# A decode step with attention and a gated feed-forward: hand-placed semaphores, three 64 KB regions and a loop on TensorE

## The chip, the core and the metric

The kernel runs on one core of a Trainium2 chip. The metric is the device time of one execution in microseconds (us). Its parts: TensorE (PE in the profile, its weight loads PEld), VectorE (DVE), ScalarE (ACT), GpSimd (POOL), SyncE (SP), which issues most of the loads, and sixteen DMA engines that carry them from HBM into SBUF.

## What is computed

One token `x` of 512 elements goes through an attention over a cache of 32,768 positions (32 query heads, 8 key/value heads, head width 128) and through a gated feed-forward of width 1792; a scalar gate mixes both. All is float32. K and V hold 134 MB each.

```
q = (x @ wq) as 32 heads of 128           # wq 512 x 4096
k, v: 8 heads, each used by 4 query heads  # 32768 x 128 each
p = softmax(q k^T / sqrt(128));  o = p v
a = o @ wo                                 # wo 4096 x 512
b = (silu(x @ w1) * (x @ w3)) @ w2         # w1, w3 512 x 1792, w2 1792 x 512
g = sigmoid(sum(x * gate_w))
out = g * a + (1 - g) * b
```

## The kernel before

The framework's tile pools place the buffers and set the semaphores; `manual_schedule` keeps each engine's instructions in the order of the program.

**Tiling.** Each K and V head is cut into four tiles of 4 MB: 128 partitions with 32 KB rows, 64 keys of 128 elements each. All tiles, both halves of wq, and w1, w3 and w2 go through the pool `stream` with four buffers (`load`, L67); each load is issued by SP as soon as the buffer's former reader is done. The eight wo pieces of 1 MB have a pool of their own with two buffers (`load_wo`, L269).

**The main loop** (L396) has 37 steps. Step i loads K tile i and, five steps behind (`LAG`), V tile i - 5. A K tile is scored in four parts (`scores`, L183): VectorE transposes a quarter of it in 32x32 blocks into a buffer `kt` (L186), and TensorE multiplies it with the head's query window `win` in four column groups (L193). ScalarE copies the finished scores to SBUF (L200).

**The chain of a head** runs between these parts. `defer` puts a function off by a number of ticks, and there are four ticks in a step: `flip` turns the scores by matmuls with a picking matrix (L209), `top` takes the maximum (L218), `maxima`, `diagonal` and `spread_max` spread it over all partitions (L228 to L240), `softmax` takes the exponentials and their sums (L250), `norm` and `invert` the reciprocal. `values` (L287) multiplies a V tile with the probabilities; after a head's last tile, `heads`, `scaled`, `quarter`, `quartered` and `mix` (L299 to L334) bring the head's output together, multiply it with its wo piece and add it to `acc`.

**Feed-forward.** w1 and w3 are loaded and used in steps 2 to 4 (`ff_rows`, L351). w2 comes last, in three pieces; `ff_down` (L432) multiplies it in two parts, around the last head's `heads`, `scaled` and `mix`. The result is written by L446.

Of the kernel before, what the change touches and what calls it, by code (L numbers as in the profile page):

```python
# [2 lines left out]

# [9 lines left out]
AX = mybir.AxisListType  # L13

P = 128
LAG = 5
# [3 lines left out]
def kernel(  # L20
    ctx: ExitStack,
    tc: tile.TileContext,
    x: bass.AP,
    k_cache: bass.AP,
    v_cache: bass.AP,
    wq: bass.AP,
    wo: bass.AP,
    w1: bass.AP,
    w3: bass.AP,
    w2: bass.AP,  # L30
    gate_w: bass.AP,
    out: bass.AP,
):
    nc = tc.nc
# [5 lines left out]
    NC = D // P  # L40
    SCALE = DH ** -0.5

    NB = 64
    UK = NB * P
    NU = S // UK
    UNITS = HKV * NU
    FR = F // P  # L50
    FJ = F // 4
    assert DH == P and D == 4 * P and REP == 4 and NU == 4 and HKV == 8 and F == FR * P

    const = ctx.enter_context(tc.tile_pool(name="const", bufs=1))
    stream = ctx.enter_context(tc.tile_pool(name="stream", bufs=4))
    proj = ctx.enter_context(tc.tile_pool(name="proj", bufs=2))
    ktp = ctx.enter_context(tc.tile_pool(name="ktp", bufs=2))
    work = ctx.enter_context(tc.tile_pool(name="work", bufs=1))
    ps_s = ctx.enter_context(tc.tile_pool(name="ps_s", bufs=2, space=bass.MemoryType.PSUM))
    ps_o = ctx.enter_context(tc.tile_pool(name="ps_o", bufs=2, space=bass.MemoryType.PSUM))  # L60
    ps_m = ctx.enter_context(tc.tile_pool(name="ps_m", bufs=4, space=bass.MemoryType.PSUM))
    ctx.enter_context(tc.manual_schedule())

    def misc(name):
        return ps_m.tile([P, 512], F32, tag="misc", name=name)

    def load(name, n, src):  # L67
        t = stream.tile([P, NB * DH], F32, tag="stream", name=name)
        nc.sync.dma_start(t[:, 0:n], src)
        return t  # L70


    xs = const.tile([P, NC], F32, name="xs")
    gw = const.tile([P, NC], F32, name="gw")
    nc.sync.dma_start(xs, x.rearrange("a b (p c) -> p (a b c)", p=P))
    nc.scalar.dma_start(gw, gate_w.rearrange("(p c) -> p c", p=P))
    wqd = wq.rearrange("(p c) n -> p (c n)", c=NC)
    QW = NC * HQ * DH // 2
    wq_t = [load(f"wq{b}", QW, wqd[:, b * QW:(b + 1) * QW]) for b in range(2)]


    ident = const.tile([P, P], F32, name="ident")
    make_identity(nc, ident)
    ones = const.tile([P, P], F32, name="ones")
    nc.vector.memset(ones, 1.0)
    sel = ident[:, 0:P:32]
    fold = const.tile([P, 32], F32, name="fold")
    nc.vector.tensor_reduce(fold, ident.rearrange("p (c r) -> p r c", c=4), axis=AX.X, op=ALU.add)

    pick = const.tile([P, 64], F32, name="pick")  # L90
    nc.vector.tensor_copy(
        pick.rearrange("p (g x) -> p g x", g=4), ident.rearrange("p (g x) -> p g x", g=4)[:, :, 0:16]
    )


    quad = const.tile([P, 4, 4, 32], F32, name="quad")
    for q in range(4):
        nc.vector.tensor_copy(quad[:, :, q, :], ident.rearrange("p (x k) -> p k x", k=4))


    xp = const.tile([P, NC, 32], F32, name="xp")
    nc.vector.memset(xp, 0.0)
    nc.vector.tensor_copy(xp[:, :, 0], xs)
    win = const.tile([P, HKV, 4, 32], F32, name="win")
    nc.vector.memset(win, 0.0)
    prob = [const.tile([P, 65 * 16], F32, name=f"prob{b}") for b in range(2)]
    otp = [const.tile([P, REP, 32], F32, name=f"otp{b}") for b in range(2)]
    for b in range(2):
        nc.gpsimd.memset(prob[b][:, 1024:1040], 0.0)
        nc.gpsimd.memset(otp[b], 0.0)  # L110
    acc = const.tile([P, P], F32, name="acc")
    nc.gpsimd.memset(acc, 0.0)
    gate = const.tile([P, 2], F32, name="gate")
    htp = const.tile([P, FR, 32], F32, name="htp")
    nc.gpsimd.memset(htp, 0.0)


    later = {}
    clock = [0]

    def defer(n, fn, *a):
        later.setdefault(clock[0] + n, []).append((fn, a))

    def tick():
        for fn, a in later.pop(clock[0], []):
            fn(*a)
        clock[0] += 1


    def gate_part():  # L130
        pr = work.tile([P, NC], F32, name="gpr")
        nc.vector.tensor_mul(pr, xs, gw)
        sm = work.tile([P, 1], F32, name="gsm")
        nc.vector.tensor_reduce(sm, pr, axis=AX.X, op=ALU.add)
        pg = misc("pg")
        nc.tensor.matmul(pg[:, 0:1], ones, sm, start=True, stop=True)
        nc.scalar.activation(gate[:, 0:1], pg[:, 0:1], AF.Sigmoid)
        nc.vector.tensor_scalar(gate[:, 1:2], gate[:, 0:1], -1.0, 1.0, op0=ALU.mult, op1=ALU.add)


    def queries():
        pq = [misc(f"pq{b}") for b in range(2)]
        for c in range(NC):
            for b in range(2):
                for j in range(4):
                    o = ((c % 2) * HKV + 4 * b + j) * REP * DH
                    nc.tensor.matmul(  # L147
                        pq[b][32 * j:32 * j + 32, :], xp[:, c, :], wq_t[c // 2][:, o:o + REP * DH],
                        start=(c == 0), stop=(c == NC - 1),
                    )  # L150
        for b in range(2):
            qs = work.tile([P, 512], F32, tag="ob", name=f"qs{b}", bufs=2)
            nc.scalar.copy(qs, pq[b])  # L153
            defer(4 * b, spread, b, qs)

    def spread(b, qs):
        rp = ktp.tile([P, 16, P], F32, tag="kt", name=f"rp{b}")
        for r in range(4):
            nc.vector.tensor_copy(  # L159
                rp[:, :, 32 * r:32 * r + 32], qs.rearrange("p (a j) -> p a j", a=16)  # L160
            )
        pt = misc(f"pt{b}")
        for a in range(16):
            nc.tensor.matmul(pt[:, 4 * a:4 * a + 4], rp[:, a, :], sel, start=True, stop=True)  # L164
        if b == 0:
            windows(b, pt)
        else:
            defer(1, windows, b, pt)

    def windows(b, pt):  # L170
        for r in range(4):
            nc.vector.tensor_copy(
                win[32 * r:32 * r + 32, 4 * b:4 * b + 4, :, 4 * r:4 * r + 4],
                pt[32 * r:32 * r + 32, 0:64].rearrange("p (q c j) -> p j c q", q=4, c=4),
            )

    recip = const.tile([P, HKV, REP], F32, name="recip")  # L180
    s_ps, sb, pf = {}, {}, {}

    def scores(i, kin, c):  # L183
        h, m = divmod(i, NU)
        kt = ktp.tile([P, NB * 32], F32, tag="kt", name=f"kt{i}_{c}")
        nc.vector.transpose(  # L186
            kt.rearrange("p (n i) -> p n i", i=32),
            kin.rearrange("p (n c j) -> p c n j", c=4, j=32)[:, c],
        )
        if c == 0:  # L190
            s_ps[0] = ps_s.tile([P, 512], F32, tag="s", name=f"s{i}")
        for g in range(4):
            nc.tensor.matmul(  # L193
                s_ps[0][32 * g:32 * g + 32, :], win[:, h, c, :], kt[:, 512 * g:512 * g + 512],
                start=(c == 0), stop=(c == 3),
            )
        if c == 3:
            if m == 0:
                sb[h] = work.tile([P, 16, 32, NU], F32, tag="sb", name=f"sb{h}", bufs=2)
            nc.scalar.copy(sb[h][:, :, :, m], s_ps[0].rearrange("p (n i) -> p n i", i=32))  # L200
            if m == NU - 1:
                mx = work.tile([P, 2, REP], F32, tag="mx", name=f"mx{h}", bufs=2)
                defer(1, flip, h, 0, mx)


    def flip(h, f, mx):
        pf[h, f] = misc(f"pf{h}_{f}")
        for a in range(8):
            nc.tensor.matmul(  # L209
                pf[h, f][:, 64 * a:64 * a + 64], sb[h][:, 8 * f + a].rearrange("p i m -> p (i m)"), pick,  # L210
                start=True, stop=True,
            )
        if f == 0:
            defer(1, flip, h, 1, mx)
        defer(1, top, h, f, mx)

    def top(h, f, mx):
        nc.vector.tensor_reduce(  # L218
            mx[:, f, :], pf[h, f].rearrange("p (n q) -> p q n", q=REP), axis=AX.X, op=ALU.max
        )  # L220
        if f == 1:
            m1 = work.tile([P, REP], F32, tag="m1", name=f"m1_{h}")
# [145 lines left out]
    def ff_up():  # L368
        defer(0, ff_turn, ff_rows("w3"))
# [105 lines left out]
```

## Time and profile before

| | us |
|---|---|
| median of 3 runs | 703.58 (703.11 to 703.68) |
| span of the profiled execution, first to last instruction | 703.1 |
| PE busy | 469.0 (67%) |
| DVE busy | 323.6 (46%) |
| ACT busy | 69.1 (10%) |
| load queue: 296.23 MB | 98.3% of 16 engines' span |

The profile is of one execution, and its span lies 0.48 us below the median of the timed runs. Instructions are grouped by the line of the kernel (L186 is line 186) and named by what they write and read (`kt<-k`). One float32 matmul of the program stands as two records of PE and two of PEld. "Idle before" a group names what ended the wait. SPq is SP's instruction stream.

### The profile page before, as it was taken

The numbers are of one execution on the slowest core, as the hardware profiler recorded it, in microseconds if no ns is written. First come the engines' busy times: TensorE is split into PE (matmuls) and PEld (weight loads), VectorE is DVE, ScalarE is ACT, GpSimd is POOL, SyncE is SP. The second block draws the span as 40 slices with busy tenths as digits, with TensorE's granted clock in tenths as the row PEclk, the third lists the DMA queues.
The fourth block names the chain that finished last, engine by engine and source line by source line (L and its number), as shares of the span: only waits on it lengthen the run. The fifth ranks groups of instructions, "written<-read, shape, count | busy, mean of one in ns | idle before, by whom it ended". The sixth has DMA issues, their size and how long they took to land.

```text
span 703.1 us, 6918 instructions
## 1 busy us (share of the span) xinstructions
PE 469.0 (67%) x3070; PEld 172.4 (25%) x3070; DVE 323.6 (46%) x269; ACT 69.1 (10%) x175; POOL 1.6 (0%) x12
## 2 busy tenths in 40 slices
PE   2776678776865499655863589635985578557746
PEld 0330143114221043113320143102331142113303
DVE  1079556654743444554543455552653556532000
ACT  0100101210200002000020003000020002000100
POOL 0000000000000000000000000000000000000000
PEclk9756656695787757976688756966678757879878
DMA  8999999999999999999999999999999999999994
GB/s 362 443 430 429 426 437 397 437 428 434 428 432 432 432 432 426 431 432 433 430 424 437 426 436 424 435 427 435 429 433 430 427 433 427 432 431 433 424 422 180
DMA packets 12085, 296.67 MB, mean 422 GB/s; under 512 B 1556, under 2 KB 1560, under 8 KB 2200
## 3 DMA queue, kind: packets, MB, share of 16 engines
q1 hardware_dynamic: 11912, 296.23, 98.3%
q8 instruction: 24, 0.39, 0.2%
q14 instruction: 5, 0.04, 0.0%
q10 hardware_dynamic: 144, 0.00, 0.0%
HBM read 296.23 MB, written 0.00 MB: 421 GB/s over the span
## 4 chain that ended last, share of the span: by engine, by line
DMA 60%; PE 20%; DVE 16%; issue 3%; ACT 0%; SPq 0%; DVEq 0%
DMA k<-in_A_k_cache_dram 47%; DVE kt L186 14%; DMA v<-in_A_v_cache_dram 10%; PE pf L209 7%; PE s L193 6%; DMA wq<-in_A_wq_dram 3%; PE o L287 3%; PE pt L164 1%; PE pa L334 1%; PE pw L351 1%; DVE mx L218 1%; PE pq L147 1%; PE ph L381 0%; PE pb L432 0%; DVE rep L376 0%
## 5 line engine op out<-in xcount | busy, mean ns | idle before, releaser
L186 DVE STREAM_TRANSPOSE kt<-k 128x2048 f32<-128x2048 f32 x128 | 289.8, 2293 | 216.2 <-DMA k<-in_A_k_cache_dram 210.6
L193 PE MATMUL s<-kt,win 128*32 128x512 f32 x1024 | 200.8, 870 | 190.5 <-DVE kt L186 183.5
L287 PE MATMUL o<-v,prob 128*32 128x512 f32 x1024 | 147.8, 729 | 14.0 <-DMA v<-in_A_v_cache_dram 14.0
L193 PEld LDWEIGHTS s<-kt,win 128*32 128x32 f32 x1024 | 25.6, 127 | 298.1 <-issue 161.1
L200 ACT COPY sb<-s 128x512 f32<-128x512 f32 x32 | 35.2, 1099 | 477.5 <-PE s L193 477.5
L287 PEld LDWEIGHTS o<-v,prob 128*32 128x32 f32 x1024 | 37.0, 133 | 113.0 <-issue 91.1
L209 PEld LDWEIGHTS pf<-pick,sb 128*128 128x128 f32 x256 | 52.5, 313 | 24.1 <-issue 24.1
L209 PE MATMUL pf<-pick,sb 128*128 128x64 f32 x256 | 55.3, 406 | 0.0
L218 DVE TENSOR_REDUCE mx<-pf 128x4 f32<-128x512 f32 x16 | 11.1, 692 | 49.6 <-PE pf L209 49.6
L250 ACT ACTIVATE prob<-pf,nm 128x128 f32<-128x128 f32 x64 | 23.4, 496 | 36.3 <-DVE nm L246 36.3
L147 PE MATMUL pq<-wq,xp 128*32 128x512 f32 x64 | 10.9, 846 | 17.8 <-DMA wq<-in_A_wq_dram 17.8
L250 ACT ACTIVATION_READ_ACCUMULATOR prob<-pf,nm 128x1 f32 x64 | 14.7, 229 | 0.0
L307 DVE TENSOR_TENSOR otp<-po,recip 128x4 f32<-128x4 f32 x1 | 0.2, 165 | 31.2 <-PE po L299 31.2
L159 DVE COPY rp<-qs 128x512 f32<-128x512 f32 x8 | 2.8, 416 | 24.0 <-ACT qs L153 24.0
L293 ACT COPY ob<-o 128x512 f32<-128x512 f32 x8 | 4.7, 587 | 76.3 <-PE o L287 76.3
L334 PEld LDWEIGHTS pa<-wo,otp 128*32 128x32 f32 x256 | 9.9, 135 | 6.3 <-issue 6.3
L334 PE MATMUL pa<-wo,otp 128*32 128x128 f32 x256 | 11.2, 328 | 0.0
L317 PEld LDWEIGHTS pk<-on,quad 128*128 128x128 f32 x56 | 9.2, 250 | 7.4 <-issue 7.3
L164 PEld LDWEIGHTS pt<-ident,rp 128*128 128x128 f32 x64 | 9.3, 235 | 3.9 <-issue 3.9
L164 PE MATMUL pt<-ident,rp 128*128 128x4 f32 x64 | 9.5, 285 | 1.1 <-DVE rp L159 1.1
L299 PEld LDWEIGHTS po<-fold,ob 128*128 128x128 f32 x64 | 7.7, 191 | 8.6 <-ACT ob L293 8.6
L317 PE MATMUL pk<-on,quad 128*128 128x4 f32 x56 | 9.8, 299 | 0.0
(57 smaller groups left out, 92.1 us busy)
## 6 DMA issues: line engine op xcount, KB each, us to landing
k<-in_A_k_cache_dram SPq DMA_DIRECT2D x32, 4096.0 KB, 29.8
v<-in_A_v_cache_dram SPq DMA_DIRECT2D x32, 4096.0 KB, 34.0
wq<-in_A_wq_dram SPq DMA_DIRECT2D x2, 4096.0 KB, 17.1
wo<-in_A_wo_dram SPq DMA_DIRECT2D x8, 1024.0 KB, 27.1
w<-in_B_w_dram SPq DMA_DIRECT2D x2, 3584.0 KB, 33.6
w<-in_B_w_dram SPq DMA_DIRECT2D x1, 2048.0 KB, 28.8
w<-in_B_w_dram SPq DMA_DIRECT2D x1, 1024.0 KB, 31.0
w<-in_B_w_dram SPq DMA_DIRECT2D x1, 512.0 KB, 31.7
```

The lines of the kernel that those rows point to most:

```text
L147: nc.tensor.matmul(pq[b][32 * j:32 * j + 32, :], xp[:, c, :], wq_t[c // 2][:, o:o + REP * DH], start=(c == 0), stop=(c == NC - 1),)
L164: nc.tensor.matmul(pt[:, 4 * a:4 * a + 4], rp[:, a, :], sel, start=True, stop=True)
L186: nc.vector.transpose(kt.rearrange("p (n i) -> p n i", i=32), kin.rearrange("p (n c j) -> p c n j", c=4, j=32)[:, c],)
L193: nc.tensor.matmul(s_ps[0][32 * g:32 * g + 32, :], win[:, h, c, :], kt[:, 512 * g:512 * g + 512], start=(c == 0), stop=(c == 3),)
L200: nc.scalar.copy(sb[h][:, :, :, m], s_ps[0].rearrange("p (n i) -> p n i", i=32))
L209: nc.tensor.matmul(pf[h, f][:, 64 * a:64 * a + 64], sb[h][:, 8 * f + a].rearrange("p i m -> p (i m)"), pick, start=True, stop=True,)
L218: nc.vector.tensor_reduce(mx[:, f, :], pf[h, f].rearrange("p (n q) -> p q n", q=REP), axis=AX.X, op=ALU.max)
L250: nc.scalar.activation(prob[h % 2][:, 0:1024].rearrange("p (a n q) -> p a n q", a=16, q=REP)[:, :, 8 * f:8 * f + 8, q], pf[h, f].rearrange ...
L287: nc.tensor.matmul(o_ps[0][32 * t:32 * t + 32, :], prob[h % 2][:, o:o + 32], vt[:, n * P:(n + 4) * P], start=(r == 0 and g == 0), stop=(r ...
L299: nc.tensor.matmul(po[:, 0:REP], ob[:, b * P:(b + 1) * P], fold[:, 4 * b:4 * b + 4], start=(b == 0), stop=(b == 3),)
L317: nc.tensor.matmul(pk[:, 4 * k:4 * k + 4], quad[:, k].rearrange("p q x -> p (q x)"), on, start=True, stop=True)
L334: nc.tensor.matmul(pa[32 * j:32 * j + 32, 0:P], otp[h % 2][:, q, :], wo_t[h][:, q, j * P:(j + 1) * P], start=(q == 0), stop=(q == REP - 1),)
```

## The change

The program is written without the framework's pools (`tile_critical`): every buffer is placed by hand and every wait is a semaphore of the kernel's own.

- **Three regions** `ra`, `rb`, `rc` of 8 MB (64 KB rows) take the place of the four stream buffers. K heads are loaded as two halves, always into ra and rb, V heads as two halves into rc, the last half of V into rb. wq uses rc first; w1 and w3 come last, into ra, then wo as a whole (two halves in ra), then w2 in four pieces in rc.
- **Keys are turned in place**: the transpose writes back into the region it reads, and TensorE reads the turned blocks with a stride of 512 bytes.
- **TensorE's work of a head is a loop** of eight passes, with branches that skip the value part in the first pass. In it, semaphores are counted down again by `take`. A pass does the scores of head h and the values of head h - 1. The other engines' instructions are written out.
- **Queries**: turned by VectorE out of PSUM and spread by sixteen copies. GpSimd copies one head's window into `winbuf` ahead of that head.
- **Softmax**: one flip of 32 half-width matmuls, one maximum, four exponentials.
- **The end**: head outputs, already scaled by the gate, are collected in `otall`. After the last head one matmul spreads them, wo and the first six rows of w2 go into one accumulator, its fold and the rest of w2 into a second, which is the result.

The new code, cut to its core:

```diff
+    def take(sem, n=1):
+        pe.wait_ge(sem, n).then_inc(sem, -n)
...
+    sp.dma_start(rc, wq.rearrange("(p c) n -> p (c n)", c=NC)).then_inc(l_q, 16)
+    sp.dma_start(ra[:, 0:half], kd[0, 0][:, 0:half]).then_inc(l_k0, 16)
+    l_a.by(sp.dma_start(ra[:, half:W], kd[0, 0][:, half:W]), 16)
+    l_b.by(sp.dma_start(rb, kd[0, 1]), 16)
+    for h in range(HKV):
+        if h < HKV - 1:
+            sp.wait_ge(c_k.sem, 2 * h + 1)
+            l_a.by(sp.dma_start(ra, kd[h + 1, 0]), 16)
+        else:
+            sp.wait_ge(c_k.sem, 2 * h + 1)
...
+        if h:
+            sp.wait_ge(c_v.sem, 2 * h)
+        else:
+            sp.wait_ge(c_dve.sem, 1)
+        sp.dma_start(rc, vd[h, 0]).then_inc(l_c, 16)
+        sp.wait_ge(c_k.sem, 2 * h + 2)
+        if h < HKV - 1:
+            l_b.by(sp.dma_start(rb, kd[h + 1, 1]), 16)
+            sp.wait_ge(c_v.sem, 2 * h + 1)
+            sp.dma_start(rc, vd[h, 1]).then_inc(l_c, 16)
+        else:
+            sp.dma_start(rb, vd[h, 1]).then_inc(l_v, 16)
+    sp.wait_ge(c_e.sem, 2)
...
+    sp.wait_ge(c_v.sem, 2 * HKV - 1)
...
+    def scores(m, region):
+        for f in range(2):
+            for c in range(4):
+                take(t_tr)
+                for g in range(4):
...
+                    i = pe.matmul(
+                        s_ps[m][32 * g:32 * g + 32, :], winbuf[:, w:w + 32],
+                        region.rearrange("p (n c i) -> p c n i", c=4, i=32)[:, c, n:n + 16],
...
+        i.then_inc(c_k.sem, 1)
...
+    with nc.Fori(0, HKV, 1, engines=[PE]) as step:
+        take(t_win, 4)
+        scores(0, ra)
+        with pe.If(step > 0):
+            norm()
+            take(l_c, 16)
+            values(0, rc)
+        scores(1, rb)
+        with pe.If(step > 0):
+            take(l_c, 16)
+            values(1, rc)
+        flips()
+        with pe.If(step > 0):
+            heads()
+        maxima()
+
+    def turned(sems, region, f):
+        for s, n in sems:
+            dve.wait_ge(s, n)
+        part = region[:, f * half:(f + 1) * half].rearrange("p (n c j) -> p c n j", c=4, j=32)
+        for c in range(4):
+            dve.transpose(part[:, c], part[:, c]).then_inc(t_tr, 1)
...
+    for h in range(HKV):
...
+        if h:
+            act.wait_ge(c_v.sem, 2 * h)
+            act.copy(ob, o_ps).then_inc(t_ob, 1)
+        dve.wait_ge(c_f.sem, h + 1)
+        dve.tensor_reduce(mx, pf.rearrange("p (a q) -> p q a", q=REP), axis=AX.X, op=ALU.max).then_inc(t_mx, 1)
...
+    take(t_e)
+    for k in range(32):
...
+    pe.wait_ge(l_w2[0], 16)
+    for k in range(W2[1]):
...
+    act.copy(ob, acc).then_inc(t_e, 1)
+    for i in range(1, 4):
+        pe.wait_ge(l_w2[i], 16)
+        for k in range(W2[i], W2[i + 1]):
+            m = rows(htp[:, k, :], w2t[:, k, :], k == W2[1], k == FR - 1)
+            if k == W2[2] - 1:
+                take(t_e)
+                rows(fold, ob, False, False)
+    dve.wait_ge(c_e.sem, n_ff + 3)
+    local.by(dve.tensor_copy(res, pb[:, 0:P]))
+    sp.dma_start(out.rearrange("a b (j e) -> (a b j) e", e=P), res[0:P:32, :]).then_inc(l_out, 16)
```

More of the change, by code (lines that the diff above doesn't have):

```diff
@@ L59 @@
[L59 to L70, printed above, removed]
@@ L73 @@
[L73 to L84, printed above, removed]
@@ L112 @@
[L112 to L138, printed above, removed]
@@ L141, in queries @@
[L141 to L149, printed above, removed]
-                    )
[L151 to L154, printed above, removed]
@@ L170, in windows @@
[L170 to L203, printed above, removed]
@@ L206, in flip @@
[L206 to L222, printed above, removed]
-            nc.vector.tensor_max(m1, mx[:, 0, :], mx[:, 1, :])
-            defer(1, maxima, h, m1)
@@ L279, in values @@
-    def values(v, vt):
-        h, r = divmod(v, NU)
-        if r == 0:
-            o_ps[0] = ps_o.tile([P, 512], F32, tag="o", name=f"o{h}")
-        for g in range(4):
-            for t in range(4):
-                o = 256 * g + 64 * r + 16 * t
-                n = 16 * g + 4 * t
-                nc.tensor.matmul(
-                    o_ps[0][32 * t:32 * t + 32, :], prob[h % 2][:, o:o + 32], vt[:, n * P:(n + 4) * P],
-                    start=(r == 0 and g == 0), stop=(r == NU - 1 and g == 3),
-                )
-        if r == NU - 1:
-            ob = work.tile([P, 512], F32, tag="ob", name=f"ob{h}", bufs=2)
-            nc.scalar.copy(ob, o_ps[0])
-            defer(0, heads, h, ob)
@@ L330, in mix @@
[L330 to L347 removed]
+    SCALE = DH ** -0.5
@@ new lines, in _program @@
+    act.dma_start(xs, x.rearrange("a b (p c) -> p (a b c)", p=P)).then_inc(l_x, 16)
+    act.dma_start(gw, gate_w.rearrange("(p c) -> p c", p=P)).then_inc(l_x, 16)
+    local = count("local")
+    n_xp = local.by(dve.memset(xp, 0.0))
+    local.by(dve.memset(ones, 1.0))
+    c_pool.by(pool.memset(ident, 0.0))
+    pool.wait_ge(c_pool.sem, c_pool.n)
+    n_ident = c_pool.by(pool.affine_select(
+        out=ident, in_=ident, compare_op=ALU.not_equal, fill=1.0, base=0, pattern=[[-1, P]], channel_multiplier=1,
+    ))
@@ new lines, in _program @@
+    dve.tensor_reduce(gsm, gpr, axis=AX.X, op=ALU.add).then_inc(t_x, 1)
+    take(t_x, 2)
+    n_gate = c_q.by(pe.matmul(mc[:, 0:1], ones, gsm, start=True, stop=True))
+    pe.wait_ge(l_q, 16)
+    for c in range(NC):
+        for b in range(2):
+            for j in range(4):
+                o = (c * HKV + 4 * b + j) * REP * DH
+                m = pe.matmul(
+                    pq[b][32 * j:32 * j + 32, :], xp[:, c, :], rc[:, o:o + REP * DH],
+                    start=(c == 0), stop=(c == NC - 1),
+                )
@@ new lines, in values @@
+    def values(r, region):
+        for g in range(4):
+            for f in range(2):
+                for t in range(4):
+                    w = 512 * r + 64 * (2 * g + f) + 16 * t
+                    n = 64 * f + 16 * g + 4 * t
+                    i = pe.matmul(
+                        o_ps[32 * t:32 * t + 32, :], prob[:, w:w + 32], region[:, n * DH:(n + 4) * DH],
+                        start=(r == 0 and g == 0 and f == 0), stop=(r == 1 and g == 3 and f == 1),
+                    )
+        i.then_inc(c_v.sem, 1)
@@ new lines, in flips, with heads @@
+    def flips():
+        take(t_ev, 2)
+        for a in range(16):
+            for s in range(2):
+                i = pe.matmul(
+                    pf[64 * s:64 * s + 64, 64 * a:64 * a + 64], sbuf[:, a].rearrange("p i m -> p (i m)"),
+                    ident.rearrange("p (gf r s q) -> p s r gf q", gf=8, r=2, s=2)[:, s],
+                    start=True, stop=True,
+                )
+        i.then_inc(c_f.sem, 1)
+    def heads():
+        take(t_ob)
+        for b in range(4):
+            i = pe.matmul(
+                mb[:, 0:REP], ob[:, b * P:(b + 1) * P], fold[:, 4 * b:4 * b + 4], start=(b == 0), stop=(b == 3)
+            )
+        i.then_inc(c_h.sem, 1)
@@ new lines, in maxima, with norm @@
+    def maxima():
+        take(t_mx)
+        pe.transpose(ma[0:REP, 0:P], mx, ident).then_inc(c_m.sem, 1)
+        take(t_md)
+        pe.matmul(ma[:, 128:128 + REP], ones[0:REP, :], md, start=True, stop=True).then_inc(c_m.sem, 1)
+    def norm():
+        take(t_p, REP)
+        pe.matmul(mc[:, 0:REP], ones, sums, start=True, stop=True).then_inc(c_n.sem, 1)
+    with nc.Fori(0, HKV, 1, engines=[PE]) as step:
[13 more added lines that the diff above has]
+        maxima()
@@ new lines, in _program @@
+    dve.wait_ge(local.sem, local.n)
+    dve.transpose(htp, hid.rearrange("p (a k) -> p k a", k=FR)).then_inc(t_e, 1)
+    norm()
+    pe.wait_ge(l_c, 16)
+    values(0, rc)
+    n_inv = inverted(HKV - 1)
+    pe.wait_ge(l_v, 16)
+    values(1, rb)
+    act.wait_ge(local.sem, n_hid)
+    act.wait_ge(c_v.sem, 2 * HKV)
+    act.copy(ob, o_ps).then_inc(t_ob, 1)
+    heads()
+    dve.wait_ge(local.sem, n_inv)
+    n = scaled(HKV - 1)
+    dve.wait_ge(local.sem, n)
+    dve.tensor_mul(
+        omask.rearrange("p (a x) -> p a x", x=4),
+        otall.unsqueeze(2).to_broadcast([P, HQ, 4]),
+        dmask.unsqueeze(1).to_broadcast([P, HQ, 4]),
+    ).then_inc(t_e, 1)
@@ L375, in ff_turn, with rows @@
+    pe.wait_ge(l_w2[0], 16)
+    for k in range(W2[1]):
+        t = k % 4
+        i = pe.matmul(
+            acc[32 * t:32 * t + 32, :], htp[:, k, :], w2t[:, k, :], start=False, stop=(k >= W2[1] - 4),
+            skip_group_check=True,
+        )
+    i.then_inc(c_e.sem, 1)
+    act.wait_ge(c_e.sem, n_ff + 2)
+    act.copy(ob, acc).then_inc(t_e, 1)
+    def rows(lhs, rhs, start, stop):
         for j in range(4):
-            nc.vector.tensor_copy(
-                rep[:, 0:FR, 32 * j:32 * j + 32], hid.rearrange("p (a k) -> p k a", k=FR)
-            )
@@ L423 @@
-    w2t = stream.tile([P, FR, D], F32, tag="stream", name="w2")
-    w2d = w2.rearrange("(p k) e -> p k e", k=FR)
-    for a, b in ((0, 8), (8, 12), (12, 14)):
-        nc.sync.dma_start(w2t[:, a:b, :], w2d[:, a:b, :])
-    pb = misc("pb")
-    def ff_down(a, b):
-        for k in range(a, b):
-            for j in range(4):
-                nc.tensor.matmul(
-                    pb[32 * j:32 * j + 32, 0:P], htp[:, k, :], w2t[:, k, j * P:(j + 1) * P],
-                    start=(k == 0), stop=(k == FR - 1),
-                )
@@ L437 @@
-    tick()
-    ff_down(0, 8)
-    tick()
-    tick()
-    tick()
-    nc.vector.tensor_scalar(acc, acc, gate[:, 0:1], None, op0=ALU.mult)
-    ff_down(8, FR)
-    res = const.tile([P, P], F32, name="res")
-    nc.vector.scalar_tensor_tensor(res, pb[:, 0:P], gate[:, 1:2], acc, op0=ALU.mult, op1=ALU.add)
-    nc.sync.dma_start(out.rearrange("a b (j e) -> (a b j) e", e=P), res[0:P:32, :])
+            i = pe.matmul(
+                pb[32 * j:32 * j + 32, 0:P], lhs, rhs[:, j * P:(j + 1) * P], start=start, stop=stop
+            )
```

389 lines of the change are left out of this document (184 added, 205 removed).

## The prediction

> **What bounds the kernel now.** I read the page first (shares, queues, chain), then the chain of waits in order of time, then the timeline and the windows of the end.
>
> ```profile
> span 703.1 us, 6918 instructions
> ...
> PE 469.0 (67%) x3070; PEld 172.4 (25%) x3070; DVE 323.6 (46%) x269; ACT 69.1 (10%) x175; POOL 1.6 (0%) x12
> ...
> q1 hardware_dynamic: 11912, 296.23, 98.3%
> ...
> DMA 60%; PE 20%; DVE 16%; issue 3%; ACT 0%; SPq 0%; DVEq 0%
> ```
>
> The load queue moves 296.23 MB, and its packets fill 98.3% of the span on sixteen engines. TensorE's and VectorE's shares of the chain are mostly work after a landing while later transfers already run. So the rate of the stream comes first. The chain shows landings as the first transposes of K tiles:
>
> ```profile
> 23.38 4.25 PE pq L147 x24
> ...
> 162.20 2.32 DVE kt L186
> ...
> 201.04 2.32 DVE kt L186
> ...
> 242.40 2.32 DVE kt L186
> ...
> 281.40 2.31 DVE kt L186
> ...
> 322.82 2.32 DVE kt L186
> ```
>
> From 201.04 to 322.82 twelve tiles of 4 MB and two wo pieces of 1 MB land, 12.5 tiles: 121.78 / 12.5 = 9.742 us each, 430.5 GB/s. All of wq (8.39 MB) had landed at 23.38. What follows up to the last V tile is 296.23 - 8.39 - 3.67 (w2) = 284.17 MB, 67.75 tiles, 660.0 us: due at 683.4.
>
> ```profile
> 687.58 6.59 PE L287 MATMUL o<-v,prob 128*32 128x512 f32 x32 [3.38 <-DMA v<-in_A_v_cache_dram]
> ...
> 694.25 0.59 ACT L293 COPY ob<-o 128x512 f32<-128x512 f32 x1 [37.74 <-PE o L287]
> ...
> 698.52 1.49 PE L432 MATMUL pb<-w,htp 128*32 128x128 f32 x48
> ...
> 700.08 0.35 DVE L445 SCALAR_TENSOR_TENSOR res<-pb,gate,acc 128x128 f32<-128x128 f32 x1 [0.70 <-PE pb L432]
> 700.46 0.65 SPq L446 DMA_DIRECT2D out_dram<-res  x1
> ```
>
> It landed at 687.58: the stream lost 4.2 us in all. Of these, 2.4 went early: the tile turned at 162.20 is 14 tiles after wq (nine of K, three of V, w1, w3 and the first wo), due at 159.8. The last 1.8 are spread over 525 us. Behind the last V tile w2 is still streaming:
>
> ```profile
> 695.00:696.00 1.00, 1.00 (x12) 0.98 (x16) 0.02 (x1) 0.00 (x0) 0.00 (x0) 1.00 0.15 61
> 696.00:697.00 1.00, 1.00 (x42) 1.00 (x42) 0.14 (x1) 0.00 (x0) 0.00 (x0) 1.00 0.00 0
> ```
>
> The last column is GB/s: the bytes end before 696. The span runs 7.1 us longer, because the values of that V tile (until 694.25), heads, wo and w2 follow one another on TensorE. So the change can gain on the start, on 4.2 us of losses and on 7.1 us of tail, unless it moves the rate.
>
> **The change, part by part.**
>
> *64 KB rows: taken at 0.* The bytes stay, the packets of K, V and wq halve. The wo pieces have 8 KB rows: four tiles with one of them (201.04 to 242.40) took 41.36 us, four without (242.40 to 281.40) 39.00. So 1 MB in four times as many packets took 2.36, no more than a quarter of a tile, 2.44; a packet's cost doesn't show. Longer rows than 32 KB the trace doesn't have; I allow 1% of the stream, -7 to +7. [...]
>
> *Start: -0.4.* wq is SP's first load, in one piece; xs goes to ACT's queue.
>
> ```profile
> 0.74 0.39 SPq L75 DMA_DIRECT2D xs<-in_A_x_dram  x1
> ...
> 1.19 0.89 SPq L69 DMA_DIRECT2D wq<-in_A_wq_dram  x2
> ...
> 2.00:3.00 1.00, 0.00 (x0) 0.00 (x0) 1.00 (x6) 0.45 (x1) 0.25 (x1) 1.00 2.01 526
> ```
>
> The row of SP's xs goes, so wq lands at about 22.95. Bytes flow 1 us after an issue (1.19 to the window from 2.00).
>
> *Three regions of 8 MB for four tiles of 4 MB.* A region takes 19.48 us. In SP's order K(0,0) has landed at 42.4 (first half 32.7), K(0,1) 61.9, K(1,0) 81.4, V(0,0) 100.9, K(1,1) 120.4, if each is issued in time. SP now waits for a whole region to be used up, and behind its waiting instruction stand all later loads: behind K(1,0) stands V(0,0), though rc is free long before; behind V(0,1) all of head 2. The prices:
>
> ```profile
> L186 DVE STREAM_TRANSPOSE kt<-k 128x2048 f32<-128x2048 f32 x128 | 289.8, 2293 | 216.2 <-DMA k<-in_A_k_cache_dram 210.6 <-PE s L193 5.5
> ...
> L200 ACT COPY sb<-s 128x512 f32<-128x512 f32 x32 | 35.2, 1099 | 477.5 <-PE s L193 477.5
> ...
> L218 DVE TENSOR_REDUCE mx<-pf 128x4 f32<-128x512 f32 x16 | 11.1, 692 | 49.6 <-PE pf L209 49.6
> ...
> L147 PE MATMUL pq<-wq,xp 128*32 128x512 f32 x64 | 10.9, 846 | 17.8 <-DMA wq<-in_A_wq_dram 17.8
> ...
> L240 PE MATMUL pb<-md,ones 4*128 4x4 f32 x16 | 3.2, 271 | 0.0
> L228 PE MATMUL pr<-ident,m 128*4 128x128 f32 x8 | 2.9, 360 | 1.0 <-DVE m L223 1.0
> ...
> L233 DVE TENSOR_REDUCE mr<-pr 4x1 f32<-4x128 f32 x8 | 2.0, 247 | 0.5 <-PE pr L228 0.4
> ...
> L172 DVE COPY win<-pt 32x64 f32<-32x64 f32 x8 | 1.8, 221 | 7.3 <-PE pt L164 7.3
> L235 DVE TENSOR_SCALAR md<-ident,mr 4x4 f32<-4x4 f32 x8 | 1.7, 217 | 0.3
> ...
> L246 DVE TENSOR_SCALAR nm<-pb 128x4 f32<-128x4 f32 x8 | 1.1, 134 | 0.3 <-PE pb L240 0.2
> ...
> L365 DVE TENSOR_TENSOR hid<-sg,pw 128x448 f32<-128x448 f32 x1 | 0.6, 622 | 0.0
> ```
>
> TensorE has two speeds here, and warms in a series: the same sixteen value matmuls took 3.64 or 6.33, sixteen records of flips 3.68 or 1.9, a group of scores 1.93, from the fourth on 1.06.
>
> ```profile
> 327.14 3.68 PE L209 MATMUL pf<-pick,sb 128*128 128x64 f32 x16
> ...
> 355.25 3.64 PE L287 MATMUL o<-v,prob 128*32 128x512 f32 x32
> ...
> 386.97 1.93 PE L193 MATMUL s<-kt,win 128*32 128x512 f32 x8 [9.11 <-DVE kt L186]
> ...
> 393.52 1.06 PE L193 MATMUL s<-kt,win 128*32 128x512 f32 x8 [0.26 <-DVE kt L186]
> ...
> 640.08 3.79 PE L209 MATMUL pf<-pick,sb 128*128 128x64 f32 x32
> ...
> 677.86 6.33 PE L287 MATMUL o<-v,prob 128*32 128x512 f32 x32 [8.73 <-DMA v<-in_A_v_cache_dram]
> ```
>
> First region, ra: wq 22.95, queries 10.9 (now after the whole of wq), two turns out of PSUM (0.6 each, as L365), sixteen small copies like L172 (3.5): 38.6. Eight transposes 18.3, last scores at most 1.9: K(1,0) is issued at 58.8 and flows from 59.8, before K(0,1) has landed (61.9). No stall, 2 us to spare.
>
> First value region, rc, the tightest: K(0,1) at 61.9, transposes 18.3, scores 1.1, copy 1.1, flips, the maximum 1.4 (twice L218), its spreading 1.2 (L228, L233, L235, L240, L246) and 0.4 for hops. Flips are now 64 records with half-width weights: between half of 2 x 3.79 and the whole, 3.8 to 7.6, I take 3.8, since the narrow weights load in step with their columns. That is 89.2; only then does VectorE turn K(1,0), landed since 81.4. Plus 18.3, scores 1.1, norm 0.4, values 7.3 (2 x 3.64): 116.3, V(0,1) flows from 117.3, against 120.4. No stall, 3.1 us to spare (-0.7 with long flips).
>
> Later heads have more. From K's landing to V's issue 18.3 + 1.1 + 0.4 + 7.3 + 1.0 = 28.1 us, while two regions cover 39.0; and from V's second landing values, flips, maximum and spreading take 14.1, plus 1 for heads, against 19.5 until the next K. DVE's in-place turn I take at 2.29, as its strided reading stands in L186 already and only the writing becomes strided; nothing shows a gain, and up to 10.9 / 8 = 1.4 us more per transpose is hidden.
>
> *Tail: -3.7.* wo, now 8 MB, lands ahead of w2 (8.5 us of stream), so V's last values, heads and spreading (28 us before the last byte) are covered, and the wo matmuls follow their half: 3.6 to 6.3 of those 8.5. After the last row of w2 there remain eight records (0.25, from the row with 48), the copy 0.35, hops 0.15 and the out DMA from 700.46 to 703.1, 2.64: 3.4 instead of 7.1. If TensorE were cold here, 2 us of it come back.
>
> *TensorE's loop, own semaphores, one accumulator: 0.* The loop names TensorE alone and has no barrier with other engines, and fewer small matmuls only free TensorE, which isn't the bound. Two waits are new. A head's scores wait for four small GpSimd copies of its query window (mean 0.13 us for GpSimd's twelve instructions now); behind them TensorE's whole head is queued, but they run while VectorE turns the first eighth, 2.3 us. On ScalarE the exponentials stand behind the copy of `ob`, which waits for the last head's values; their own input, the spread maximum, comes after those values anyway. If either cover were gone, it would be under 1 us a head, inside the 10.9 above. On SP, wo waits for both feed-forward matmuls on ra, over 25 us ahead of its turn in the stream.
>
> **The sum.** 22.95 + 287.84 MB in 68.63 tiles, 668.6, + 1.8 of lost stream (the early 2.4 gone with the longer queue) + tail 3.4 = 696.8 us of span, against 703.1. The median of the runs, 703.58, lies 0.48 above this profiled execution's span, so **697.3 us**.
>
> **Rivals.**
>
> *Cold TensorE on the first pass (slower).* In the first value chain TensorE idles before the flips and again before K(1,0). Cold, it costs 1.8 on scores (two groups at 1.94 for 1.06), 5.4 on values (12.7 for 7.3), and on flips 3.6, or 10.9 if half-width weights gain nothing (14.7 for 3.8): 10.8 to 18.1 against 3.1 of slack. The stream then stands 7.7 to 15.0 us, 705.0 to 712.3; in the middle 708.7. It is slower as soon as the chain grows by more than 10.8, and every further us is paid whole. For it: 677.86. Against it: eight groups of scores precede each, and the third warms them.
>
> *The jump back stalls TensorE (slower).*
>
> ```profile
> q8 instruction: 24, 0.39, 0.2%
> ...
> gw<-in_gate_w_dram ACTq DMA_DIRECT2D x1, 2.0 KB, 2.0
> ...
> w<-in_B_w_dram SPq DMA_DIRECT2D x1, 512.0 KB, 31.7
> ```
>
> The program itself arrives by DMA in 24 packets, and a loop goes back to code it has left. A jump then costs a small load, between 2.0 us (gw) and 31.7, if it queues like w2's piece. From the end of one head's spreading there are 34.7 us until its scores have to be done, of which warming scores take 11.1: a stall up to 23.6 us is hidden. At 31.7 it costs 8.1 in each of seven heads, 754 us. [...]
>
> *In-place turns are slower.* At twice 2.29 the chain of 28.1 becomes 46.4, 7.4 over its cover in seven heads: 749. It decides from 3.65 us each.
>
> *The gain is eaten (no change).* Handing over 8 MB regions loses 5 to 7 us more, by the long flips, a skipped branch at head 0 and a cold tail: 702.2 to 705.0.
>
> *The rate rises by 1% with long rows (faster):* 690.4.
>
> **How the numbers follow.** Forecast 0.56, rate 0.08, no change 0.10, cold first pass 0.15, jump 0.06, in place 0.05. A measurement here tells 0.2% from no change: faster means below 702.2, slower above 705.0. Faster 0.64, same 0.10, slower 0.26. The range 691 to 709 takes in the forecast with its bounds, half of the higher rate and the cold pass up to its middle; jump, in-place turns and those other halves, some 0.2, stay out.
>
> **What would show it.** Right: load queue full from 2 us on, first halt none around 118 to 122, turns of 2.3 us, the bytes ending near 693 and out issued 1 us later. Wrong: a hole in the GB/s line at 120, turns over 3.6 us, a first score group that waits for nothing after each head, or slices well off 430 GB/s.

## The result, and the profile after

The change makes the kernel faster: 698.65 us median (697.92 to 699.55, four runs) against 703.63 (703.11 to 704.51) on the same chip, a ratio of 0.993 with a 95% interval of 0.9916 to 0.9944. The forecast was 697.3. The profiled execution took 698.76 us, its span is 696.7; forecast was a span of 696.8. That hit is partly luck, as the stages below show: a halt that wasn't forecast and a faster stream that wasn't either cancel. The gain in time was forecast at 6.3 us and is 5.0.

The page of the changed kernel (busy time by engine, GB/s in 40 slices of 17.4 us, queues):

```profile
span 696.7 us, 6587 instructions
...
PE 374.5 (54%) x2944; PEld 104.0 (15%) x2944; DVE 307.9 (44%) x208; ACT 38.7 (6%) x94; POOL 7.1 (1%) x41
...
GB/s 399 412 453 411 430 419 369 421 425 467 433 421 421 421 478 425 421 421 433 463 429 421 421 433 463 429 421 421 433 463 429 422 421 433 426 459 426 425 419 276
...
q1 hardware_dynamic: 6056, 296.23, 98.6%
q8 instruction: 6, 0.10, 0.1%
```

Same bytes, half the packets, and 6 packets of code where there were 24. The stream is full but for the seventh slice (369), the start and the end. Landings, as the first transposes of regions in the timeline (start, duration, what ended the wait):

```profile
61.89 17.66 DVE L295 STREAM_TRANSPOSE rb<-rb 128x2048 f32<-128x2048 f32 x8 [4.46 <-DMA rb<-in_A_k_cache_dram]
...
122.02 8.89 DVE L295 STREAM_TRANSPOSE rb<-rb 128x2048 f32<-128x2048 f32 x4 [10.79 <-DMA rb<-in_A_k_cache_dram]
...
162.69 17.66 DVE L295 STREAM_TRANSPOSE ra<-ra 128x2048 f32<-128x2048 f32 x8 [4.36 <-DMA ra<-in_A_k_cache_dram]
...
317.81 17.66 DVE L295 STREAM_TRANSPOSE ra<-ra 128x2048 f32<-128x2048 f32 x8 [7.30 <-DMA ra<-in_A_k_cache_dram]
...
511.31 8.89 DVE L295 STREAM_TRANSPOSE rb<-rb 128x2048 f32<-128x2048 f32 x4 [21.04 <-DMA rb<-in_A_k_cache_dram]
```

K(0,1) lands at 61.9 to the tenth as worked out. K(1,1) comes 1.6 late (120.4 was due), K(2,0) 3.3 late (159.4). From then on the stream makes good: from 317.81 to 511.31 five pairs of regions take 193.50, 38.70 us a pair, where two regions were put at 38.96 and the kernel before took 39.00 for its four tiles without wo.

Half of the 3.3 us (1.66, by the first experiments below) went in the first head's flips and what follows them:

```profile
82.17 0.65 PE L248 MATMUL psum<-ident,sbuf 128*64 128x64 f32 x14 [0.82 <-PEq L106]
87.68 3.04 PE L248 MATMUL psum<-ident,sbuf 128*64 128x64 f32 x50 [4.85 <-issue]
...
93.58 17.65 DVE L295 STREAM_TRANSPOSE ra<-ra 128x2048 f32<-128x2048 f32 x8
...
113.52 7.83 PE L238 MATMUL psum<-rc,prob 128*32 128x512 f32 x64
121.42 0.33 SPq L134 DMA_DIRECT2D rc<-in_A_v_cache_dram  x1
...
153.29 2.08 PE L248 MATMUL psum<-ident,sbuf 128*64 128x64 f32 x64
...
189.27 0.33 SPq L134 DMA_DIRECT2D rc<-in_A_v_cache_dram  x1
```

TensorE stops for 4.85 us after 14 of 64 records, and no semaphore is named: "issue". The trace's list of DMA packets has one packet of TensorE's code (queue q8, 16 KB) from 85.28 to 86.18 us, and the flips go on at 87.68. In every later head the flips are one run (2.08 us at 153.29). The whole chain behind shifts, V(0,1) is issued at 121.42 instead of 116.3, and the stream stands (last column GB/s). A hole at 120 was the prediction's own sign of being wrong:

```profile
119.00:120.00 1.00, 1.00 (x16) 0.35 (x12) 0.00 (x0) 0.00 (x0) 0.00 (x0) 1.00 0.31 131
120.00:121.00 1.00, 1.00 (x16) 0.12 (x6) 0.00 (x0) 0.00 (x0) 0.00 (x0) 1.00 0.00 0
```

One head later the same issue comes at 189.27, 12 us ahead of its turn. The end:

```profile
684.30 5.34 PE L404 MATMUL psum<-ra,oq 128*32 128x512 f32 x32 [3.81 <-DMA ra<-in_A_wo_dram]
...
693.48 0.29 DVE L435 COPY res<-psum 128x128 f32<-128x128 f32 x1 [16.78 <-PE psum L421]
693.79 0.64 SPq L437 DMA_DIRECT2D out_dram<-res  x1
```

The out DMA is issued at 693.79, where it was 700.46; 2.9 us follow it. By the trace's landing times the last piece of w2 is there at 692.92, so the bytes end near 693 and out is issued 0.9 us later, both as forecast.

### The profile page after: what moved, and what is told of

Read it like the earlier page. It is cut to its first block, busy times and chain, and to the rows that moved or that the text cites. A ratio compares the mean times of both kernels' runs of the same rounds, so it can differ in the third digit from the quotient of the medians.

```text
span 696.7 us, 6587 instructions
## 1 busy us (share of the span) xinstructions
PE 374.5 (54%) x2944; PEld 104.0 (15%) x2944; DVE 307.9 (44%) x208; ACT 38.7 (6%) x94; POOL 7.1 (1%) x41
## 5 line engine op out<-in xcount | busy, mean ns | idle before, releaser
L295 DVE STREAM_TRANSPOSE rb<-rb 128x2048 f32<-128x2048 f32 x64 | 141.8, 2275 | 141.5 <-DMA rb<-in_A_k_cache_dram 141.5
L225 PE MATMUL psum<-rb,winbuf 128*32 128x512 f32 x512 | 96.7, 835 | 133.6 <-PEq L106 133.5
L295 DVE STREAM_TRANSPOSE ra<-ra 128x2048 f32<-128x2048 f32 x64 | 141.3, 2274 | 39.6 <-DMA ra<-in_A_k_cache_dram 39.6
L225 PE MATMUL psum<-ra,winbuf 128*32 128x512 f32 x512 | 93.0, 801 | 106.0 <-PEq L106 106.0
L238 PE MATMUL psum<-rc,prob 128*32 128x512 f32 x960 | 114.8, 633 | 20.8 <-DMA rc<-in_A_v_cache_dram 16.5
L238 PEld LDWEIGHTS psum<-rc,prob 128*32 128x32 f32 x960 | 34.4, 116 | 96.5 <-issue 79.9
L225 PEld LDWEIGHTS psum<-rb,winbuf 128*32 128x32 f32 x512 | 13.6, 124 | 213.3 <-issue 213.3
L248 PE MATMUL psum<-ident,sbuf 128*64 128x64 f32 x512 | 18.3, 233 | 5.7 <-issue 4.9
L342 ACT ACTIVATE prob<-psum,nm 128x256 f32<-128x256 f32 x32 | 18.9, 701 | 41.1 <-DVE nm L339 41.1
L248 PEld LDWEIGHTS psum<-ident,sbuf 128*64 128x64 f32 x512 | 17.0, 146 | 13.1 <-issue 13.1
```

What stands on the lines that cost most here:

```text
L225: i = pe.matmul(s_ps[m][32 * g:32 * g + 32, :], winbuf[:, w:w + 32], region.rearrange("p (n c i) -> p c n i", c=4, i=32)[:, c, n:n + 16], ...
L238: i = pe.matmul(o_ps[32 * t:32 * t + 32, :], prob[:, w:w + 32], region[:, n * DH:(n + 4) * DH], start=(r == 0 and g == 0 and f == 0), stop ...
L248: i = pe.matmul(pf[64 * s:64 * s + 64, 64 * a:64 * a + 64], sbuf[:, a].rearrange("p i m -> p (i m)"), ident.rearrange("p (gf r s q) -> p s ...
L295: dve.transpose(part[:, c], part[:, c]).then_inc(t_tr, 1)
L342: act.activation(prob[:, 0:1024].rearrange("p (a n q) -> p n a q", a=16, q=REP)[:, :, :, q], pf.rearrange("p (n a q) -> p n a q", n=16, q= ...
```

## Experiments

**The hole in the first head's flips.** The eight passes written out, without loop and branches:

```diff
-    with nc.Fori(0, HKV, 1, engines=[PE]) as step:
+    for step in range(HKV):
...
-        with pe.If(step > 0):
+        if step > 0:
```

> TensorE's eight passes written out, no loop and no branches; all else as in the changed kernel. Theory: the 4.85 us hole inside the first head's flips (from 82.8 to 87.7 us, behind the skipped value part) is TensorE waiting for code after a branch; it makes V(0,1) late and the stream stand at 119 to 122. Without branches the first flips are one run of 2 to 4 us, V(0,1) is issued near 116.5 instead of 121.4, the hole in the GB/s line at 120 is gone, and the span falls by 1.7 to 3 us: time about 696.3. The instruction queue goes from 6 packets to some 23. Rival: the hole comes from the clock or from the copy before it and stays, and the loop's fewer instruction packets are worth something: time 698.7 or up to 1 us more.

Measured: the hole is gone, but the kernel is slower than the changed one: 701.25 us (699.93 to 702.65), 0.9964 of before (0.995 to 0.9978). Timeline:

```profile
81.48 2.08 PE L248 MATMUL psum<-ident,sbuf 128*64 128x64 f32 x64 [0.81 <-PEq L106]
...
113.36 0.33 SPq L134 DMA_DIRECT2D rc<-in_A_v_cache_dram  x1
...
277.05 8.89 DVE L295 STREAM_TRANSPOSE rb<-rb 128x2048 f32<-128x2048 f32 x4 [21.05 <-DMA rb<-in_A_k_cache_dram]
...
316.82 17.66 DVE L295 STREAM_TRANSPOSE ra<-ra 128x2048 f32<-128x2048 f32 x8 [8.27 <-DMA ra<-in_A_k_cache_dram]
```

V(0,1) is issued at 113.36, 8 us earlier, and K(2,0) lands 1.9 us earlier, at 160.82. Then the gain is lost on the way: the pair that ends at 316.82 took 39.77 instead of 38.70. (This trace is of the fastest of the five executions, 699.93 us.) Both theories got one half: without the branches there is no hole in this trace, and writing out costs something the theory had at nothing. The next run takes only the branches away:

```diff
+    take(t_win, 4)
+    scores(0, ra)
+    scores(1, rb)
+    flips()
+    maxima()
-    with nc.Fori(0, HKV, 1, engines=[PE]) as step:
+    with nc.Fori(1, HKV, 1, engines=[PE]):
...
```

> The first head's pass stands ahead of the loop without its value part, and the loop runs seven times without any inner branch. Theory (only the skipped code costs, jumping back is free): as written out, hole gone, V(0,1) issued near 116.5, time about 696.3, with 7 to 9 instruction packets. Rival (jumping back costs on the way too): slower than the written-out version by 0.5 us or more, or holes at the start of heads.

Measured: 696.73 us (695.74 to 698.34), 0.9905 of before (0.989 to 0.992); on another chip, expected as

> The version with the first head ahead of the loop once more, unchanged, as the measure for the other two on the same chip: 696.7, 0.990 of the kernel before.

it was 696.89, 0.9903 (0.9886 to 0.992). In the first one's timeline the hole is gone, and V(0,1) is issued 5 us ahead of the landing of K(1,1):

```profile
82.72 3.68 PE L248 MATMUL psum<-ident,sbuf 128*64 128x64 f32 x64 [0.79 <-PEq L106]
...
117.10 0.33 SPq L134 DMA_DIRECT2D rc<-in_A_v_cache_dram  x1
...
122.34 8.89 DVE L297 STREAM_TRANSPOSE rb<-rb 128x2048 f32<-128x2048 f32 x4 [15.43 <-DMA rb<-in_A_k_cache_dram]
```

In the trace of its second measurement a hole of 1.56 us is back, after 19 records:

```profile
82.44 1.30 PE L248 MATMUL psum<-ident,sbuf 128*64 128x64 f32 x19 [0.80 <-PEq L106]
85.29 2.62 PE L248 MATMUL psum<-ident,sbuf 128*64 128x64 f32 x45 [1.56 <-issue]
```

So the branch isn't needed for a hole, and the packets of code tell why. In all eight traces with a hole, the flips go on 1.3 to 1.5 us after the end of one packet of TensorE's code; here it ran from 82.88 to 83.89. In the four traces without a hole this packet had come before the flips began, at 75.36 in the first measurement of this version and at 77.27 in the written-out one. With the branch the hole is 2.50 to 4.85 us in four traces; without it, it is 0 to 2.37 in seven, and 6.17 in one with more code on the way. TensorE waits for code that is late, and in these traces it waits longer with the branch.

Jumping back costs nothing visible. This version is 1.9 us below the changed kernel and 4.5 below the written-out one, with the same first head, and no other came out clearly faster.

**Code on the way.** What differs between the last two is the code that is loaded: 23 packets against 7. So code was added elsewhere, on GpSimd, that has nothing else to do:

```diff
             ).then_inc(t_win, 1)
+        for _ in range(540):
+            pool.wait_ge(c_pool.sem, 1)
```

> The version with the first head ahead of the loop, and behind each head's four window copies on GpSimd 540 waits that are met already: about 4,300 instructions of an engine that has nothing else to do, some 17 more instruction packets of 16 KB, as many as TensorE's written-out program has more. No data moves otherwise. Theory: each packet holds one DMA engine for about 1 us, and a region has landed only when its slowest engine is done, so the packets themselves made the written-out version slower: time 699.5 to 701.5, against 696.7 without, with landings falling behind in steps of 0.3 to 1 us. Rival: the written-out version is slower because TensorE itself waits for code: no change here, 696.7.

Measured: 704.75 us (703.97 to 707.63), 1.0021 of before (1.001 to 1.0031), 7.9 slower than without on the same chip, more than expected. The trace is of the slowest of twelve executions, 707.63 us, and has 2,161 more instructions, half of what was expected. Its queues, two landings and its first flips, with the longest hole of all:

```profile
q8 instruction: 7, 0.11, 0.1%
q14 instruction: 20, 0.16, 0.1%
```

```profile
323.04 17.66 DVE L300 STREAM_TRANSPOSE ra<-ra 128x2048 f32<-128x2048 f32 x8 [7.86 <-DMA ra<-in_A_k_cache_dram]
...
480.47 17.66 DVE L300 STREAM_TRANSPOSE ra<-ra 128x2048 f32<-128x2048 f32 x8 [7.84 <-DMA ra<-in_A_k_cache_dram]
```

```profile
83.33 1.30 PE L251 MATMUL psum<-ident,sbuf 128*64 128x64 f32 x19 [0.81 <-PEq L107]
90.80 2.62 PE L251 MATMUL psum<-ident,sbuf 128*64 128x64 f32 x45 [6.17 <-issue]
```

GpSimd's code came in 16 more packets, of 8 KB, on another queue. Four pairs took 157.43, 39.36 each, 0.66 too much, and that looks even only because most pairs hold one such packet. Region by region it is in steps, as the theory had it. The trace has sixteen ends for every load, one for each engine's share. From 224.28 to 500.47 us, regions took 20.0 us from landing to landing where a packet of GpSimd's code fell into them and 19.35 where none did. The last of the sixteen ends comes 0.24 us behind the second last at 165.81, 1.73 at 303.00, 4.19 at 460.44 and 6.85 at 617.90, while the others keep their step. So it is one engine that falls back, and the kernel waits for it. To tell loading from executing, the same waits in a loop:

```diff
+        with nc.Fori(0, 18, 1, engines=[mybir.EngineType.Pool]):
+            for _ in range(30):
+                pool.wait_ge(c_pool.sem, 1)
```

> As the version with 540 met waits a head on GpSimd, but these stand in a loop of 18 passes of 30: as many instructions are executed, a tenth of the code is loaded. Theory A (loading the code slowed the stream, 704.75 against 696.9): the time comes back to 696 to 698, and GpSimd's instruction packets fall from 20 to about 6. Theory B (executing or recording 4,300 more instructions slowed it): 704 to 706 as before.

Measured: 696.56 us (696.49 to 697.13), 0.990 (0.9883 to 0.9917). The trace has 2,456 more instructions than without, so no fewer are executed, and the 8 us are gone:

```profile
q8 instruction: 7, 0.11, 0.1%
...
q14 instruction: 4, 0.03, 0.0%
```

So it is loading the code, not running it. A dose between the two for TensorE, three passes written out and four in the loop:

> First head ahead, three passes written out, then TensorE's loop for the last four heads. Theory (TensorE's code packets slow the stream, about 0.28 us each by 4.5 us for 16): some 8 packets more than with the first head alone ahead of the loop, time 698.5 to 699.5. Rival (writing out costs in another way, or only beyond what TensorE can hold): 696.9 as with one head ahead, or 701 as written out whole.

Measured: 698.92 us (697.72 to 701.84), 0.9935 (0.9914 to 0.9956), with 15 packets. 7, 15 and 23 packets give 696.7, 698.9 and 701.25: about 2.2 us for eight. These packets, too, cost in steps (the pair of 39.77 above), but they don't pile up on one engine: written out, the last end of a load stays within 0.4 us of the second last from 102 us on, while the first runs up to 5.4 us ahead.

**Row length.** Every 8 MB load issued as two of 32 KB rows, in the changed kernel and in the version with the first head ahead:

```diff
-            l_a.by(sp.dma_start(ra, kd[h + 1, 0]), 16)
+            l_a.by(sp.dma_start(ra[:, 0:half], kd[h + 1, 0][:, 0:half]), 16)
+            l_a2.by(sp.dma_start(ra[:, half:W], kd[h + 1, 0][:, half:W]), 16)
```

> Each 8 MB load is issued as two loads of 32 KB rows (the two halves of each partition's row) into the same regions, and the reader waits for both: row length and number of loads are as before the change, the ring of three regions stays. Theory A (long rows are worth nothing, the steadier stream comes from the longer queue): regions keep landing every 19.40 us in the middle, time 698.0 to 699.0; gate_w lands earlier, near 13 us. Theory B (long rows are worth 0.4%): 19.48 us a region as before the change, time 700.5 to 701.5.

> The version with the first head ahead of the loop, every 8 MB load issued as two of 32 KB rows. Theory: a pair of regions lands every 38.86 us instead of 38.70, over 17 pairs 2.7 us: time about 699.2. Rival (the difference of the earlier run was its halt at 120 and the chip): no change within 0.7 us, 696.7.

Measured: 699.9 us (699.13 to 700.25), 0.9942 (0.9928 to 0.9955), and 698.3 (697.77 to 700.25), 0.9926 (0.991 to 0.9941), 1.4 us above the same version with 64 KB rows on that chip. Landings of the second:

```profile
317.46 17.66 DVE L307 STREAM_TRANSPOSE ra<-ra 128x2048 f32<-128x2048 f32 x8 [6.42 <-DMA ra<-in_A_k_cache_dram]
...
511.75 8.89 DVE L307 STREAM_TRANSPOSE rb<-rb 128x2048 f32<-128x2048 f32 x4 [21.18 <-DMA rb<-in_A_k_cache_dram]
```

Five pairs in 194.29: 38.86 each, in both runs. In the first run cadence and time lie between the two theories (38.80 and 38.96 a pair); in the second the cadence is the one expected, and the time half of it. Long rows gain 0.16 us a pair, 0.4%. Each load also became two, and the runs don't separate the length of the rows from the number of loads.

**The start.** The small loads landed late:

```profile
xs<-in_A_x_dram ACTq DMA_DIRECT2D x1, 2.0 KB, 7.6
...
gw<-in_gate_w_dram ACTq DMA_DIRECT2D x1, 2.0 KB, 24.2
```

The queries wait for both. With x first on SP's queue:

> Only x goes back to SP's queue ahead of wq, so that gate_w is alone and first on ScalarE's queue; nothing else is changed. Theory: the small loads landed late (7.6 and 24.2 us after issue) because each of their rows took turns with wq's 64 KB rows. Issued first, both land near 3 us, the queries start at about 23.4 instead of 26.1, K(1,0) is issued near 56.2 instead of 58.7, and the dip at 59 to 63 us goes. But V(0,1)'s chain starts from the landing of K(0,1), so the halt at 120 stays: time 697.3 to 698.7. Rival: the late start is passed on whole, 2.6 us less: 696.0.

Measured: 699.18 us (698.6 to 700.77), 0.9929 (0.9916 to 0.9943), 0.5 above the theory's range. Both small loads land within 2 us of their issue, the queries start at 23.54 and K(1,0) is issued at 57.48. There is no gain in time, as the theory had it: V(0,1) is issued no earlier (123.37, behind a hole of 4.30 us), so the stream's second halt stays.

**The tail.** Sixteen extra matmuls into an unused bank keep TensorE busy between wo's halves:

> Sixteen extra matmuls into an unused PSUM bank fill TensorE's wait between the two halves of wo. Theory: TensorE was cold after that wait and worked the second half in 5.34 us, so that the end ran up to 2 us behind the last bytes. Kept warm it takes 3.64, the last matmuls then wait for w2's last piece, and out is issued 0.7 to 1.7 us earlier: time 697.3. Rival: w2's last piece lands no earlier than the work ends now: no change, 698.7.

Measured: 699.94 us (698.46 to 702.44), 0.995 (0.9932 to 0.9967): not faster. The rival holds. In this run the second half of wo takes 3.64 us, and TensorE waits at the end for w2:

```profile
692.26 1.08 PE L428 MATMUL psum<-rc,sbuf 128*32 128x128 f32 x32 [0.57 <-DMA rc<-in_B_w_dram]
```

It waits for the third piece of w2, which landed at 692.22 (692.28 in the changed kernel). The fourth landed at 692.85, before TensorE came to it, and is used in the same go. So 1.08 us of work stand behind the third piece's landing, warm or cold. On the kernel before, the last landing was changed instead:

```diff
+            if v == UNITS - 1:
...
             vt = load(f"v{v}", NB * DH, vd[v])
```

> The kernel before with one thing moved: w2's three loads are issued ahead of the last V tile instead of behind it. Same bytes, other last landing. Theory (what stands behind the last landing sets the tail): the last V tile lands near 696, and its values (3.6 to 6.6), copy, heads, wo and the sums follow, some 12 us with the out load: span about 708.5, time 709. Rival (the end is the stream's end plus a fixed part): no change, 703.6.

Measured: 712.4 us (711.89 to 713.25), 1.0124 of before (1.0104 to 1.0144).

```profile
696.02 5.41 PE L287 MATMUL o<-v,prob 128*32 128x512 f32 x32 [12.29 <-DMA v<-in_A_v_cache_dram]
...
707.71 0.65 SPq L447 DMA_DIRECT2D out_dram<-res  x1
```

The V tile lands at 696.02, and the span ends 14.4 us later, at 710.4. Same bytes, 8.7 us more: the landing came where it was expected, and the work behind it took 14.4 us instead of 12. What stands behind the last landing is paid in full.

**Together**, first head ahead, x first and warm tail:

> First head ahead of the loop, x first, warm tail, together on the changed kernel. Theory: the three add up: no halt at 120, K(1,0) issued near 56, out issued about 1 us behind the last bytes: time 694 to 695.5. Rival: they share one slack and give no more than the best of them alone, 696.3.

Measured: 696.99 us (695.1 to 699.21), 0.990 (0.9879 to 0.992), no better than the first alone. The rival holds.

## Why the prediction was right, and where it wasn't

- **Rate of the stream, taken at 0: wrong by 0.4%.** The wo pieces were a poor witness: 1 MB in 2.36 us couldn't show 0.16 in 38.86. The rest of the way from the forecast 38.96 to 38.70 isn't the rows' (two loads of 32 KB rows take 38.86). In the changed kernel pairs land every 38.70 us, 433.5 GB/s, against 430.5 before. The 1% that the prediction allowed either way was its author's estimate; the runs show 0.7%.
- **TensorE's loop, taken at 0: the largest error.** Written out, the program with the same first head is 4.5 us slower. The prediction asked only what TensorE would do with the time, and not what its code costs the loads, though the row with 24 packets was quoted.
- **First value region, 3.1 us of slack: wrong.** The terms themselves held (18.3 for transposes was 17.7, values 7.3 were 7.8, the maximum 1.4 was 1.2, flips 3.8 were 3.7 together). The narrow weights did load faster, though not in step with their columns: one load of the flips took 138 ns with 64 columns and 192 with 128 at the faster of TensorE's two speeds, 227 and 333 at the slower. What lacked was the 4.85 of waiting for code, named only in the rival without change, as a skipped branch. V(0,1) came 5.1 late, and without the branch the kernel gains 1.9. That a jump costs a small load was the author's estimate. Behind the skipped branch the hole was 2.50 to 4.85 us, though a hole also comes without it, 1.56 us in the trace above. For the jumps back no run shows it: from 94.5 to 628.8 us no packet of TensorE's code comes, and the loop runs without such a hole.
- **The cold first pass** came in part: flips take 2.1 warm and 3.7 cold (written out, and with the first head ahead), both within the 3.8 put in, and the first values take 7.1 to 7.9 (9.1 with x first) for 7.3. That is at most 1.8 us over the sum, not the 10.8 that the rival needed.
- **First region, later heads, in-place turns: right.** K(1,0) was issued at 58.69 (58.8 forecast), though by errors that cancel: the queries began at 26.6 instead of 22.95, as gate_w came late, and took 8.6 instead of 10.9. Later heads have 12 us (10.9). An in-place turn takes 2.275 us (2.29).
- **Lost stream, 1.8: wrong in place.** 3.1 us were lost by 201, of which the hole is 1.7 (199.74 without it), and next to nothing after. The rest went at K(1,0): half of its engines were done by 81.20, with the forecast 81.4, but the last one at 83.31.
- **Tail, 3.4 from the last byte: 3.8.** The last byte landed at 692.92. The work left at the third piece's landing, 0.64 earlier, takes 1.08 and sets the end, and the out DMA takes 2.9 (2.64). Before, the last byte landed at 696.24, not ahead of 696, which leaves 6.9. So the tail saved 3.1 instead of 3.7.
- **What lies around the span, 0.48: wrong.** The prediction set the span of one execution, 703.1, against the median of others, 703.58. Where span and time of the same execution of the kernel before are known, they are 701.8 and 703.62, 1.8 apart, and a span of 703.1 belongs to a time of 704.88. After the change it is 2.06. This alone makes up the 1.4 between 697.3 and 698.65.

So the sum of the span is right to 0.1 because +3.1 (early stream), +0.4 (tail) and +0.3 (wo and w2, 28.3 for 28.0) stand against -1.9 (cadence, 23.9 regions at 19.405 for 19.484 up to the last V region) and the 1.8 that were not lost again. Direction and size come from the steps that were right: the stream stays the bound, the ring of three holds in the later heads, the tail shrinks.

Open: why a packet of GpSimd's code, which itself takes 0.31 us, sets its engine back by 0.65, and why all of them fall on one engine. Also the parts don't add up across kernels: written out, the changed kernel loads as much code as the kernel before and is only 2.5 us faster, less than tail and rows together.

## What to carry to other kernels

When the DMA queues are the bound, count everything that rides on them: the program's own code is a load as well (7, 15 and 23 packets of TensorE's gave 696.7, 698.9 and 701.25 us), and a loop can be worth more than what the engine itself saves. A region was there when its slowest engine was done, with GpSimd's code on the way up to 6.85 us after the next, so look for what rides on one engine alone. Look at the first pass of a ring, where buffers are still filling and code is still missing (4.85 us in the changed kernel), apart from the steady passes. And put last into the stream what needs the least work after it lands: the span ended 14.4 us after the last landing where that was a V tile, and 3.8 where it was 0.26 MB of w2.

## What the runs showed of the hardware

- Sixteen more packets of TensorE's code (0.27 MB of 296) cost 4.5 us, sixteen of GpSimd's (0.13 MB) 7.9; in a loop GpSimd's cost nothing (696.56 us against 696.89).
- GpSimd's packets set one of the sixteen engines back, 0.65 us a packet, until its share of a load ended 6.85 us behind the next.
- TensorE stopped in its first flips until 1.3 to 1.5 us after a late packet of its code: 2.50 to 4.85 us with a branch ahead, 0 to 2.37 without (6.17 with GpSimd's code on the way). On the jumps back no packet of its code came, from 94.5 to 628.8 us, and there was no such hole.
- A 2 KB load issued just behind a load of 64 KB rows landed 24.2 us after its issue; before, ahead of it, 2.0.
- Rows of 64 KB instead of 32 KB, in half as many loads: 38.70 against 38.86 us for 16.8 MB.
